# A banded-attention and feed-forward kernel gets a new planner, fixed PSUM pieces, wider loads and a split last tile

## The chip, the cores and the metric

The kernel runs on one core of a Trainium2 chip. The metric is the device time of one execution in microseconds (us). The engines named below are TensorE (PE in the profile, PEld for its weight loads), VectorE (DVE), ScalarE (ACT), GpSimd (POOL) and the sync engine (SP), which only issues transfers. Each engine works through its own instructions in the order in which they were emitted.

## The reference

Attention over 4 sequences of 768 tokens, 8 heads of 64, each query seeing the 96 tokens up to itself and the first 8 tokens of the sequence, with a bias that falls with distance at a slope of its own per head; then a feed-forward layer without skip:

```python
scores = scale * np.matmul(q, k.transpose(0, 1, 3, 2))
keep = is_global | is_local                       # first 8 tokens, or 0 <= rel < 96
dist = np.where(is_global & ~is_local, 96.0, np.abs(rel))
scores = np.where(keep, scores - slopes * dist, -1e9)
a = softmax(scores)
x = (a @ v) as 3072 rows of 512
h = x @ w_in                                      # 512 -> 2048
out = (h - np.tanh(h)) @ w_out                    # 2048 -> 512
```

All inputs and the output are float32; the kernel's matmuls take bfloat16.

## The kernel before, in words

**Tiles.** The 3072 tokens are 24 tiles of 128 tokens, six to a sequence. A tile needs the keys of itself and of the tile before it, so it has two score blocks, `o=0` (diagonal) and `o=1` (off-diagonal); the first tile of a sequence has only the diagonal one, which makes 44 blocks. The 8 global keys and values are copied into the first rows of each later tile (`a_K`, `a_V`), so that the off-diagonal block covers them too.

**One tile's way.** `load` fetches k, q and v (256 KB each, line 143) by SP. `cast` (line 157) turns k and q to bfloat16, on GpSimd except for tile 0. k and q are transposed: for tiles 0 to 7 by TensorE (`a_T`, line 169, eight 128x128 transposes into one PSUM bank) with copies out by ScalarE and VectorE (`a_Te`, 180 and 182), from tile 8 on by a transposing transfer (`a_DT`, line 173). `a_S` (line 190) makes one block of scores: 8 matmuls of 128 columns, one per head, into a two-bank PSUM piece. `a_E` (198, ScalarE) takes the exponential; `a_M` (202, VectorE) multiplies it by `mk`, the exponential of bias and mask. `a_AV` (213 and 217) multiplies by v, with a column of ones for the row sums; `a_R` (225 and 226) divides; `a_X` and `a_Xe` (240, 249), from tile 9 on `a_DX` (252), transpose the result into `xT`. So much is the attention.

**The feed-forward part.** `m1` (line 273) multiplies by `w_in` into one PSUM bank, `m1_th` (284, ScalarE) takes tanh, `m1_g` (290, VectorE) subtracts. The first six tiles go one by one (four blocks of 128 columns fill a bank: 16 matmuls of 128 columns), the rest in threes (one block of 384 columns: 4 matmuls). `m2` (300) multiplies by `w_out`, in four quarters of four matmuls of 512 columns; `m2_e` (307) copies out, `store` (310) writes 256 KB.

**Weights.** `w_in` and `w_out` come in four pieces of 1 MB each (lines 149 and 152, issued by GpSimd and cast on the way). Weights and the early tiles share one list, `before`: tiles 0 to 3, the four pieces of `w_in`, the four of `w_out`, then tiles 4, 5, 6. An entry of that list waits for the landing of the one two places ahead of it (except between neighbouring tiles).

**The order.** Every step is put down by `op` with its engine, an assumed duration, what it follows (`after`) and which buffers it takes and gives. `plan` walks through them: again and again it takes the step that can start first, with a priority for ties, and so fixes the order on each engine before anything runs. m1 and m2 (priority 2) fill up TensorE. `with_warm` then adds matmuls on zeros (`warm`, line 265) wherever TensorE is planned idle up to 19 us. PSUM is two pools: two pieces of two banks, shared by score blocks and AV results, and four single banks for all else; a pool hands out its pieces in turn.

**The start.** Ahead of the planned steps, VectorE builds the distances and masks in `rmat` (lines 92 to 104) from a GpSimd iota and sets the ones of v, and ScalarE makes `mk` of it by 8 exponentials (line 107).

Of the kernel before, what the change touches and what calls it, by code (L numbers as in the profile page):

```python
# [8 lines left out]
FP32 = mybir.dt.float32  # L9
# [7 lines left out]
def kernel(  # L17
# [30 lines left out]
    PE_T, PE_X = 8, 9  # L48
    HT = 3


    EARLY, EARLY2 = 6, 4
# [17 lines left out]
    ident = cpool.tile([P, P], BF16, name="ident")  # L70
    mk = cpool.tile([P, H, 3, P], BF16, name="mk")
    rmat = cpool.tile([P, 3, P], FP32, name="rmat")
    tmp01 = cpool.tile([P, 2, 2, P], FP32, name="tmp01")
# [4 lines left out]


    def slot(h):  # L80
        return (h % 2) * NP + h // 2


    def build_masks():


        r = rmat[:, 1:3, :]
# [5 lines left out]
            out=tmp01[:, 0], in0=r, scalar1=0.0, scalar2=BIG, op0=ALU.is_lt, op1=ALU.mult  # L93
        )
        nc.vector.tensor_scalar(
            out=tmp01[:, 1], in0=r, scalar1=float(L), scalar2=BIG, op0=ALU.is_ge, op1=ALU.mult
        )
        nc.vector.tensor_tensor(out=r, in0=r, in1=tmp01[:, 0], op=ALU.max)
        nc.vector.tensor_tensor(out=r, in0=r, in1=tmp01[:, 1], op=ALU.max)
# [4 lines left out]
        nc.vector.memset(rmat[0:G, 2, :], float(L))  # L104
        for h in range(H):
            slope = 2.0 ** (-8.0 * (h + 1) / H)
            nc.scalar.activation(mk[:, slot(h), :, :], rmat, AF.Exp, bias=0.0, scale=-slope)


    ops = {}  # L110
    w_in_r = moe_w_in.rearrange("(c p) f -> p c f", p=P)
    w_out_r = moe_w_out.rearrange("(c p) d -> p c d", p=P)
    PE, ACT, DVE, POOL, SP = ENG.PE, ENG.Activation, ENG.DVE, ENG.Pool, ENG.SP

    LAT = {PE: 0.17, ACT: 0.1, DVE: 0.1, POOL: 0.12, SP: 0.0}

    def op(key, eng, us, fn, after=(), take=(), give=(), pri=0, dma=0.0):
        ops[key] = dict(
            key=key, eng=eng, us=us, fn=fn, after=[a for a in after if a is not None],
            take=list(take), give=list(give), pri=pri, dma=dma,  # L120
        )

# [12 lines left out]


    kf, qf, vf = {}, {}, {}
    kq = {}

    def load(u, nm, src, dst):  # L140
        b, i = u // NQ, u % NQ
        dst[u] = stpool.tile([P, H, Dh], FP32, name=nm)
        started(("ld", nm, u), nc.sync.dma_start(  # L143
            out=dst[u], in_=src[b, :, i * P : (i + 1) * P, :].rearrange("h p d -> p h d")
        ))
# [410 lines left out]
```

## Time and profile before

| | |
|---|---|
| runs | 225.67 us median of 3 (224.74 to 227.08) |
| profiled execution, first to last instruction | span 224.4 us; its time with what lies around the span is not listed |
| TensorE busy | 211.9 us, 94% of the span; 11.5 us of it on zeros (line 265) |
| VectorE, ScalarE, GpSimd busy | 136.4, 124.2, 53.8 us |
| first feed-forward matmul | 21.44 us |
| last matmul to the end | 220.8 to 224.4 us |

A busy TensorE is the union of its matmuls' spans, so time lost between matmuls that overlap isn't seen in it; the start-to-start time is read from the chain. The profile's waits name what ended an engine's idle time.

### The profile page before, as it was taken

The page shows a single profiled execution, that of the slowest core. Times are in us where ns is not written, and L with a number is a line of the kernel's source. Part 1 is how long each engine was busy: PE and PEld are TensorE (multiplying, and loading weights), DVE is VectorE, ACT ScalarE, POOL GpSimd, SP SyncE. Part 2 cuts the span into 40 slices and gives each one's busy share as a digit, 9 for nine tenths or more (in the row PEclk, how much of TensorE's full clock was granted, in tenths as well). Part 3 has the DMA queues.
Part 4 walks back from the last instruction along what each step waited for, and adds up shares of the span by engine and source line. Part 5 has one row for each costly group of instructions (what it writes and reads, how often), then busy time and mean ns, then how long its engine had stood idle before and what let it go on. Part 6 is the DMA issues. An engine that isn't in the chain of part 4 may idle for free.

```text
span 224.4 us, 5020 instructions
## 1 busy us (share of the span) xinstructions
PE 211.9 (94%) x1975; PEld 126.0 (56%) x1998; DVE 136.4 (61%) x279; ACT 124.2 (55%) x205; POOL 53.8 (24%) x85
## 2 busy tenths in 40 slices
PE   6898899999899999899999999999999999999993
PEld 2455897555785565445555555555555555555541
DVE  5367785215898599743897767677675743444300
ACT  5655654256775487543778384746664644544321
POOL 1473212064463432233233332322000000000000
PEclk9999999999999999999999999999999999999999
DMA  7999999999999999999999999997514121011112
GB/s 151 219 207 152 151 191 164 221 204 290 240 190 201 189 265 194 193 200 196 250 240 198 206 187 234 223 170 150 120 33 107 50 70 47 3 48 47 47 49 95
DMA packets 107640, 35.85 MB, mean 160 GB/s; under 512 B 100448, under 2 KB 104544, under 8 KB 107616
## 3 DMA queue, kind: packets, MB, share of 16 engines
q1 hardware_dynamic: 103392, 31.34, 72.3%
q0 software_dynamic: 4224, 4.19, 12.1%
q8 instruction: 15, 0.25, 0.5%
q14 instruction: 9, 0.07, 0.1%
HBM read 27.26 MB, written 6.29 MB: 150 GB/s over the span
## 4 chain that ended last, share of the span: by engine, by line
PE 78%; DMA 7%; SPq 6%; DVE 3%; ACT 3%; issue 1%
PE one L273 35%; PE one L300 34%; SPq L143 5%; PE big L190 4%; DMA w_in_bf_97<-in_moe_w_in_dram 3%; DMA vf<-in_v_dram 3%; PE big L213 2%; PE big L217 2%; DMA xT<-x 2%; ACT pd L198 2%; DVE po L202 1%; DVE pd L202 1%; PE one L240 1%; PE one L169 1%; DVE xT L249 1%
## 5 line engine op out<-in xcount | busy, mean ns | idle before, releaser
L284 ACT ACTIVATE th<-one 128x384 f32<-128x384 f32 (+1 forms) x120 | 60.7, 516 | 51.7 <-PE one L273 47.7
L290 DVE TENSOR_TENSOR g<-one,th 128x384 bf16<-128x384 f32 (+1 forms) x120 | 67.6, 579 | 32.7 <-ACT th L284 30.7
L300 PEld LDWEIGHTS <-g 128*128 128x128 bf16 x384 | 36.0, 98 | 36.0
L198 ACT ACTIVATE pd<-big 128x1024 bf16<-128x1024 f32 x24 | 24.6, 1024 | 16.6 <-PE big L190 14.9
L157 POOL CAST kq<-kf 128x512 bf16<-128x512 f32 x23 | 14.8, 645 | 56.7 <-DMA kf<-in_k_dram 46.6
L307 ACT COPY ot<-one 128x512 f32<-128x512 f32 x24 | 14.1, 587 | 23.9 <-PE one L300 23.8
L202 DVE TENSOR_TENSOR pd<-pd,mk 128x1024 bf16<-128x1024 bf16 x24 | 18.4, 768 | 11.9 <-ACT pd L198 11.5
L273 PE MATMUL one<-xT,w_in_bf_96 128*128 128x128 bf16 (+1 forms) x192 | 24.6, 273 | 1.1 <-DVE xT L249 0.9
L273 PE MATMUL one<-xT,w_in_bf_97 128*128 128x128 bf16 (+1 forms) x192 | 24.7, 273 | 0.8 <-DMA w_in_bf_97<-in_moe_w_in_dram 0.8
L273 PE MATMUL one<-xT,w_in_bf_99 128*128 128x128 bf16 (+1 forms) x192 | 25.2, 273 | 0.0
L273 PE MATMUL one<-xT,w_in_bf_98 128*128 128x128 bf16 (+1 forms) x192 | 25.1, 273 | 0.0
L300 PE MATMUL one<-w_out_bf_100,g 128*128 128x512 bf16 x88 | 24.1, 379 | 0.5 <-issue 0.2
L300 PE MATMUL one<-w_out_bf_103,g 128*128 128x512 bf16 x94 | 24.1, 379 | 0.2
L300 PE MATMUL one<-w_out_bf_101,g 128*128 128x512 bf16 x92 | 23.8, 379 | 0.2
L300 PE MATMUL one<-w_out_bf_102,g 128*128 128x512 bf16 x89 | 23.1, 379 | 0.4 <-issue 0.2
L198 ACT ACTIVATE po<-big 128x1024 bf16<-128x1024 f32 x20 | 20.5, 1025 | 1.4 <-PE big L190 1.4
L273 PEld LDWEIGHTS <-w_in_bf_96 128*128 128x128 bf16 x192 | 14.6, 98 | 9.1 <-issue 1.3
L273 PEld LDWEIGHTS <-w_in_bf_99 128*128 128x128 bf16 x192 | 14.8, 98 | 7.4
L273 PEld LDWEIGHTS <-w_in_bf_97 128*128 128x128 bf16 x192 | 14.4, 98 | 7.9 <-DMA w_in_bf_97<-in_moe_w_in_dram 1.0
L273 PEld LDWEIGHTS <-w_in_bf_98 128*128 128x128 bf16 x192 | 14.6, 98 | 7.2
L157 POOL CAST kq<-qf 128x512 bf16<-128x512 f32 x23 | 15.6, 678 | 10.0 <-DMA qf<-in_q_dram 9.9
L202 DVE TENSOR_TENSOR po<-po,mk 128x1024 bf16<-128x1024 bf16 x20 | 15.9, 797 | 3.0 <-ACT po L198 3.0
(91 smaller groups left out, 181.2 us busy)
## 6 DMA issues: line engine op xcount, KB each, us to landing
kf<-in_k_dram SPq DMA_DIRECT2D x24, 256.0 KB, 4.0
qf<-in_q_dram SPq DMA_DIRECT2D x24, 256.0 KB, 4.4
vf<-in_v_dram SPq DMA_DIRECT2D x24, 256.0 KB, 4.8
out_dram<-ot SPq DMA_DIRECT2D x24, 256.0 KB, 2.9
w_in_bf_96<-in_moe_w_in_dram POOLq DMA_DIRECT2D x1, 512.0 KB, 6.4
w_in_bf_97<-in_moe_w_in_dram POOLq DMA_DIRECT2D x1, 512.0 KB, 6.5
w_in_bf_98<-in_moe_w_in_dram POOLq DMA_DIRECT2D x1, 512.0 KB, 6.6
w_in_bf_99<-in_moe_w_in_dram POOLq DMA_DIRECT2D x1, 512.0 KB, 5.3
```

What stands on the lines that cost most here:

```text
L143: started(("ld", nm, u), nc.sync.dma_start(out=dst[u], in_=src[b, :, i * P : (i + 1) * P, :].rearrange("h p d -> p h d")))
L157: eng.tensor_copy(out=kq[u][:, j, :], in_=src.pop(u).rearrange("p h d -> p (h d)"))
L190: nc.tensor.matmul(s[:, slot(2 * p + hh), :], qk[u - o][r, 1, p, :], qk[u][r, 0, p, :], start=True, stop=True,)
L198: nc.scalar.activation(pr[u, o], s, AF.Exp, bias=0.0, scale=scale)
L202: nc.vector.tensor_tensor(out=pr[u, o], in0=pr[u, o], in1=mk[:, :, m, :], op=ALU.mult)
L213: nc.tensor.matmul(dst, pr[u, 0][:, slot(h), :], vb[u % NV][:, h, :], start=True, stop=last,)
L217: nc.tensor.matmul(dst, pr[u, 1][:, slot(h), :], vb[(u - 1) % NV][:, h, :], start=False, stop=True,)
L273: nc.tensor.matmul(t[:, (f - f0) * n : (f - f0 + 1) * n], w_in_bf[j][:, c, fo : fo + P], xT[b][:, c, o : o + n], start=(c == 0), stop=(c = ...
L284: nc.scalar.activation(h_view(ths[g, f0], g), h_view(hs[g, f0], g), AF.Tanh, bias=0.0, scale=1.0)
L290: nc.vector.tensor_tensor(out=gs[b][:, f0 : f0 + m, o : o + n], in0=h_view(hs.pop((g, f0)), g), in1=h_view(ths.pop((g, f0)), g), op=ALU.su ...
L300: nc.tensor.matmul(os_[u], gs[u // HT][:, f, t * P : (t + 1) * P], w_out_bf[f // FJ][:, f % FJ, :], start=(f == 0), stop=(f == CF - 1),)
L307: nc.scalar.copy(out=ots[u], in_=os_.pop(u))
```

## The change

- **PSUM pieces.** The two pools go. Two fixed pairs of banks (`pairs`) and four fixed banks (`ones`) are allocated once, and the planner itself assigns which piece each step gets (`got`, `bank`).
- **Planner.** `plan` now follows the two queues of transfers (SP's and GpSimd's) as first-in-first-out lists that share the rate by weights, has other durations and latencies, and for a step of the attention on TensorE compares with 0.3 us added to its readiness once feed-forward work has begun (`MARGIN`).
- **Score blocks.** From tile 5 on the first block takes both pairs, and the second takes none and has priority -9; it is planned after the first one's end.
- **Loads.** k and q of tiles 0 to 8 are loaded with 4 tokens (1 KB) per descriptor in place of one (256 bytes); cast and the copies out of the transposes put the rows in order. Those nine tiles (before: eight) are transposed by TensorE, k and q each in a bank of its own, four transposes each.
- **Order of loads.** Tiles 0 to 4, then `w_in` 0 and 1, `w_out` 0 and 1, `w_in` 2, tile 5, `w_out` 2, `w_in` 3, `w_out` 3, tiles 6 and 7; again each waits for the entry two places ahead.
- **Bias.** In tiles 0 and 1 (three blocks) TensorE adds bias and mask to the scores by 8 matmuls more a block (`a_B`), and `a_M` is left out there. `mk` is made by eight planned steps on ScalarE. The diagonal mask is made on GpSimd (`affine_select`), and the ones of v are set by GpSimd.
- **Last tile.** Its `w_out` product is made in two halves of 256 columns, copied out by ScalarE and VectorE and stored apart.
- **Matmuls on zeros.** The planner's limit goes from 19 to 16 us; 18 are emitted where there were 42.

```diff
-    ps_big = ctx.enter_context(tc.tile_pool(name="ps_big", bufs=2, space=bass.MemoryType.PSUM))
-    ps_one = ctx.enter_context(tc.tile_pool(name="ps_one", bufs=4, space=bass.MemoryType.PSUM))
+    pairs = [psum.tile([P, 2, 512], FP32, name=f"pair{i}") for i in range(2)]
+    ones = [psum.tile([P, 512], FP32, name=f"one{i}") for i in range(4)]
...
+        if nm != "v" and u < PE_T:
+            s = src.rearrange("(a c) (t j) d -> t a c (j d)", c=2, j=J4)
+            i = nc.sync.dma_start(out=t.rearrange("p (c j) d -> p c (j d)", c=2), in_=s)
...
+    def a_Te(u, j, eng):
+        b = half(ones[bank(("T", u, j))])[:, 0 : NP * P]
+        i = b.rearrange("p (j t a) -> p a t j", j=J4, a=NP)
+        o = qk[u][:, j].rearrange("p a (t j) -> p a t j", j=J4)
...
+    def a_B(u, o):
+        s = scores(u, o)
+        for h in range(H):
+            nc.tensor.matmul(
+                s[:, slot(h), :], sid[:, h, :], rbf[:, dist_of(u, o), :],
+                start=(slot(h) % NP == 0), stop=False, skip_group_check=True,
+            )
...
-    AHEAD = 5.0
-    WARM = (1.4, 19.0)
-    before = [("t", 0), ("t", 1), ("t", 2), ("t", 3), ("in", 0), ("in", 1), ("in", 2), ("in", 3),
-              ("out", 0), ("out", 1), ("out", 2), ("out", 3), ("t", 4), ("t", 5), ("t", 6)]
+    AHEAD = 5.5
+    WARM = (1.3, 16.0)
+    MERGE = 5
+    SEQ = ["t0", "t1", "t2", "t3", "t4", "i0", "i1", "o0", "o1", "i2", "t5", "o2", "i3", "o3", "t6", "t7"]
+    LAG = 2
...
+            both = u >= MERGE and i
+            for o in (0, 1) if i else (0,):
+                take = [("pair", ("S", u, 0)), ("pair", ("S", u, 1))] if both else [("pair", ("S", u, o))]
+                take = [] if both and o else take
+                deps = te + [("K", u - 1) if o and i >= 2 else None, ("S", u, 0) if o else None]
...
+                op(("S", u, o), PE, (0.24 if both else 0.4) if o or both else 0.4, lambda u=u, o=o: a_S(u, o),
+                   after=deps, take=take, pri=-9 if both and o else 0)
...
+                late = r
+                if o["eng"] is PE and o["pri"] == 0 and first_m[0] is not None and r > 0:
+                    late = r + MARGIN
+                c = (round(max(f, late), 3), o["pri"], n)
...
+    def l2(qq, c):
+        for f in range(qq * 4, qq * 4 + 4):
+            nc.tensor.matmul(
+                ones[bank(("l2", 0, c))][:, 0:HC], gs[u // HT][:, f, u % HT * P : (u % HT + 1) * P],
+                w_out_bf[f // FJ][:, f % FJ, c * HC : (c + 1) * HC], start=(f == 0), stop=(f == CF - 1),
+            )
```

More of the change, by code (lines that the diff above doesn't have):

```diff
@@ L419, in plan @@
[L419 to L426 removed]
+    make_ops()
+    BUFS = {"pair": 2, "one": 4, "mo": 3, "sk": 4, "sq": 4, "sv": 4, "kq": 3, "p0": 3, "p1": 3,
+            "x": 3, "xT": 4, "g": 3, "th": 3, "ot": 4}
@@ L427, in plan @@
+    START = {PE: WARM[0], ACT: 2.1, DVE: 3.3, POOL: 3.3, SP: 0.75}
+    LAT = {PE: 0.21, ACT: 0.04, DVE: 0.06, POOL: 0.06, SP: 0.0}
+    MARGIN = 0.3
+    RING = 3 * 1024
+    def plan():
+        avail = {n: [(0.0, i) for i in range(c)] for n, c in BUFS.items()}
+        free = dict(START)
+        done = {("dist",): 3.2}
+        start = {}
+        avail["one"][3] = (WARM[1], 3)
+        fifo = {SP: [], POOL: []}
+        clock = [0.0]
         f1 = f2 = 0.0
         queues = {}
-        for u in range(NU):
+        for u in range(NU - 1):
```

515 lines of the change are left out of this document (319 added, 196 removed).

## The prediction

> **What bounds the kernel now.** I read the page's shares first, then busy time by stage, then the waits, the order of time and the chain.
>
> ```profile
> span 224.4 us, 5020 instructions
> PE 211.9 (94%) x1975; PEld 126.0 (56%) x1998; DVE 136.4 (61%) x279; ACT 124.2 (55%) x205; POOL 53.8 (24%) x85
> ...
> L265 PE MATMUL one<-zero 128*128 128x512 bf16 x40 | 11.5, 425 | 1.4 <-DVE zero L514 1.2 <-issue 0.2
> ...
> 15.00:20.00 5.00, 4.27 (x54) 2.46 (x52) 3.66 (x9) 2.62 (x3) 3.30 (x5) 1.00 1.06 163
> 20.00:25.00 5.00, 3.79 (x74) 3.22 (x73) 3.90 (x9) 3.15 (x4) 0.75 (x2) 1.00 1.09 174
> 50.00:60.00 10.00, 8.90 (x134) 6.54 (x132) 6.29 (x13) 7.02 (x10) 5.06 (x7) 1.00 1.16 272
> 60.00:70.00 10.00, 9.64 (x160) 7.84 (x158) 9.72 (x19) 5.78 (x9) 4.17 (x6) 1.00 1.13 190
> 80.00:100.00 20.00, 18.75 (x190) 10.56 (x191) 15.06 (x33) 12.61 (x22) 5.63 (x10) 1.00 1.20 208
> 140.00:160.00 20.00, 19.84 (x171) 11.04 (x173) 13.84 (x28) 13.11 (x22) 5.20 (x7) 1.00 0.93 178
> ...
> 21.44 1.96 PE L273 MATMUL one<-xT,w_in_bf_96 128*128 128x128 bf16 x32
> ...
> PE one L273 <- DMA w_in_bf_97<-in_moe_w_in_dram: 0.8, 1, 0.8
> PE big L217 <- DVE po L202: 1.2, 3, 0.7
> ...
> 220.82 0.59 ACT ot L307
> ```
>
> TensorE bounds it. In a settled stretch (140 to 160 us) it idles 0.16 us in 20, the background that I expect of any plan. So the span splits in four: 21.44 us until the first feed-forward matmul, of which 11.5 us are matmuls on zeros; the work after that; the waits in it; and 3.6 us from the last matmul (220.8) to the end. The waits: 0.8 us for the second piece of w_in, 1.10 + 0.36 us between 50 and 70 us, and 1.25 us between 80 and 100 us, where a value product stands at the head of TensorE until the masked scores (line 202) are ready. The profiled execution's own time isn't listed, so the sum is made on its span; the median of the runs lies 1.27 us above that, and I add the sum to the median.
>
> **The change part by part.**
>
> *First feed-forward matmul.* It waits for the first piece of w_in, which waits for a tile to land.
>
> ```profile
> 6.45 0.61 POOL L160 CAST vb_104<-vf 128x512 bf16<-128x512 f32 x1 [4.83 <-DMA vf<-in_v_dram]
> 10.07 0.73 POOL L160 CAST vb_105<-vf 128x512 bf16<-128x512 f32 x1 [0.60 <-DMA vf<-in_v_dram]
> 13.93 0.88 POOL L149 DMA_DIRECT2D w_in_bf_96<-in_moe_w_in_dram  x1 [0.84 <-DMA vf<-in_v_dram]
> 18.19 0.75 POOL L149 DMA_DIRECT2D w_in_bf_97<-in_moe_w_in_dram  x1 [1.25 <-DMA vf<-in_v_dram]
> 20.59 0.74 POOL L149 DMA_DIRECT2D w_in_bf_98<-in_moe_w_in_dram  x1 [1.04 <-DMA w_in_bf_96<-in_moe_w_in_dram]
> ...
> 27.53 0.74 POOL L152 DMA_DIRECT2D w_out_bf_100<-in_moe_w_out_dram  x1 [1.80 <-DMA w_in_bf_98<-in_moe_w_in_dram]
> 30.55 0.74 POOL L152 DMA_DIRECT2D w_out_bf_101<-in_moe_w_out_dram  x1 [2.29 <-DMA w_in_bf_99<-in_moe_w_in_dram]
> 33.59 0.74 POOL L152 DMA_DIRECT2D w_out_bf_102<-in_moe_w_out_dram  x1 [2.29 <-DMA w_out_bf_100<-in_moe_w_out_dram]
> ```
>
> Tiles land 3.62 us apart (6.45 to 10.07), 1.21 us per 256 KB in pieces of 256 bytes. No row has 1 KB pieces on SP's queue. Upper bound 1.21 us (a larger piece has no reason to cost more); lower bound the weights, whose 1 MB lands every 3.03 us, 0.76 us per 256 KB. I take 0.8, nearest the weights, also long pieces. A tile then takes 0.8 + 0.8 + 1.2 = 2.8 us: the first lands at 5.65, the fourth at 14.05, the fifth at 16.85. The first w_in piece now waits for the fourth tile instead of the third, so it is issued at 14.05 where it was 13.93, and with the same 6.66 us lands near 20.6. The first matmul goes from 21.44 to about 20.6: **-0.8** (from -1.5 to +2.5, the last if the wide loads cost 1.21). The Trainium skill, "DMA: Bandwidth & Descriptors", section Specifications, wants at least 512 bytes per descriptor for full rate; at its 27 GiB/s per engine 256 KB would take an estimated 0.57 us, which would put the fourth tile at about 12.2 us.
>
> What else could be late then is ScalarE.
>
> ```profile
> 0.74 1.28 ACT L107 ACT_TABLE_LOAD   x1 [0.74 <-PEq L537]
> 3.75 3.41 ACT L107 ACTIVATE mk<-rmat 128x384 bf16<-128x384 f32 x8 [1.72 <-DVE rmat L104]
> L198 ACT ACTIVATE pd<-big 128x1024 bf16<-128x1024 f32 x24 | 24.6, 1024 | 16.6 <-PE big L190 14.9 <-DVE vb_106 L232 1.8
> L180 ACT COPY qk<-one 128x512 bf16<-128x512 bf16 x8 | 4.7, 583 | 1.1 <-PE one L169 1.1
> ```
>
> In the changed program the table load waits for VectorE's distances (about 3.1 us), where it ran free at 0.74; behind it queue all ScalarE work. Up to the fifth tile's copy ScalarE has 1.28 + 3.41 + 5 x 0.58 + 7 x 1.02 = 14.7 us, so that copy ends at 17.8 without a gap. The two score blocks of the fifth tile, which stand before the first feed-forward matmul on TensorE, follow it by about 19.5. Weights at 20.6 cover that by 1 us; beyond, each late microsecond is paid. The bias matmuls (three blocks) and the strided copies out fall before 20.6 and replace matmuls on zeros: 0. GpSimd's eight scalings of 128 columns, a quarter each of the 0.61 us that its casts of 512 take (row at 6.45), and eight small memsets are some 2 us ahead of its first cast at 5.65: 0; at the full 0.61 us each they would push that cast by 2 us, into ScalarE's margin.
>
> *TensorE work after that point.* By the emitted orders, before has 38 score blocks left in 26 runs; after has 35 blocks in 35 runs. So "in one run" isn't what comes out: the second block is planned after the end of the first, and feed-forward work that can start sooner slips between each pair. What a run costs:
>
> ```profile
> 36.34 0.86 PE one L300 x4
> 37.20 0.89 PE one L273 x16
> ...
> 48.96 0.55 PE big L190 x16
> 49.52 0.97 PE one L300 x4
> ...
> 57.77 0.33 PE big L190 x8
> 58.10 1.00 PE one L273 x16
> ```
>
> One block takes 0.33 us, two together 0.55, and the group behind any run takes 0.11 more (0.97 for 0.86, 1.00 for 0.89). So a block costs 0.22 and a run 0.22 on top. Nine runs more, +1.98; three blocks fewer, -0.66; one transpose of x fewer (4 x 0.0556), -0.22. Four tiles' q and k transposes remain in both. **+1.1** (0.7 to 1.4).
>
> *The second w_in piece.* Issued when the fifth tile lands (16.85), it is through 3.0 us behind the first, 23.6. TensorE has until then three groups of 16 on piece one (2.7) and two value products: the 0.8 us wait goes, **-0.8**.
>
> *The third w_in piece.* It used to be third, now two w_out pieces are ahead of it. w_out 0 is issued at 20.6 and lands at 26.6 (27.53 to 33.59 was 6.06), the third w_in piece is issued then and lands at 32.7. TensorE until then has ten groups of 16 (8.9), two value products (0.5 each), two transposes of x and one quarter of w_out (0.86), 11.2 us from 20.6, plus some 0.4 us of waits for banks, since VectorE's subtractions stand in a line with divisions there. It arrives at 32.2. Wait 0.5 + 0.4, **+0.9** (0 to +4: tile 5's loads start near 30 and share the rate).
>
> *Starvation at 50 to 70 us.*
>
> ```profile
> 39.24 0.37 SPq L143 DMA_DIRECT2D kf<-in_k_dram  x1
> ```
>
> Tile 4 was first asked for at 39.24. Now tiles 4 and 5 come before that, and tile 6 starts when w_in 3 has landed, near 41. A tile's feed-forward work is 4 x 0.89 + 4 x 0.86 = 7.0 us (rows of the chain above), two tiles 14, less the 1.8 us later start: 12 us more cover. 1.46 - 0.16 of background: **-1.3** (0 to -1.4).
>
> *80 to 100 us.* The waits on line 202 total 1.2 us. The new planner prefers filler where attention would be less than 0.3 us ready, with TensorE's latency set longer; that is about the size of each wait but the longest. But a tile now holds both pairs from its first block. Between nothing and -1.1 I take **-0.6**.
>
> *Tail.*
>
> ```profile
> DMA to landing us min/median/max: 2.0/2.9/4.5
> 1.86 0.29 DVE L95 TENSOR_SCALAR tmp_94<-rmat 128x256 f32<-128x256 f32 x1
> ```
>
> Copy 0.59, then 3.0 us for the last store. Half the columns on VectorE take about 0.3 (256 columns took 0.29), half the bytes between 2.0 and 3.0, say 2.7. **-0.6** (-0.2 to -1.3). The first half hides under the second's matmuls.
>
> Sum: -0.8 + 1.1 - 0.8 + 0.9 - 1.3 - 0.6 - 0.6 = **-2.1**; span 222.3, and 225.67 - 2.1 = **223.6**. The new order from 100 us on I cost at nothing: there TensorE idles so little that it can hardly gain, and other engines have the cover of their shares above (61%, 55%, 24%); should it lose, that is part of the forecast's upper side.
>
> **The rivals.**
>
> 1. *The new order waits nowhere.* The 0.9 doesn't come, the waits at 80 to 100 us go fully (-0.5 more), and the last store is as short as the shortest one (-0.7 more): -4.2, 221.5. For it: 0.16 us per 20 us in settled stretches shows TensorE can be kept so. Against: piece three arrives by my sum later than it is wanted.
> 2. *The wide loads buy nothing* (1.21 us each). Fourth tile at 17.3, first piece at 23.9, first matmul 3.3 us later than forecast: +1.2, 226.9. Against it: the weights' 0.76.
> 3. *TensorE runs dry at piece three, and the clock falls.*
>
> ```profile
> 1.20 3.63 PE L265 MATMUL one<-zero 128*128 128x512 bf16 x9 [1.20 <-DVE zero L514]
> 5.94 1.89 PE L265 MATMUL one<-zero 128*128 128x512 bf16 x8
> ```
>
> The first matmuls of 512 columns come 0.43 us apart, those after 5 us 0.216. If tile 5's loads go ahead of piece three by a whole tile (2.8 us), TensorE stands 3.4 us; the pieces behind are late by as much, about 1.5 us more; and if the clock then falls to the rate of the first row, the next 3.6 us do half work, 1.8 us. -2.1 + 2.8 + 1.5 + 1.8 = +4.0, 229.7. It decides when piece three lands after 35.5 us. For it: 18 matmuls on zeros where there were 42, in-order weights. Against: an even share would cost only a third of it. The Trainium skill, "TensorE: Matmul & The Clock Gate", Part 1, says that an idle window of about 3.4 us halves the clock until about as long a busy one has passed; the two rows agree with the ramp, no row here shows the fall.
>
> **How the numbers follow.** Forecast 0.46 (222.3 to 225.0), rival 1 0.30, rival 2 0.10, rival 3 0.14. Runs differ by 1% among themselves, so 1% (223.4, 227.9) is about what can be told. Faster: all of rival 1 and nearly half of the forecast, 0.51; slower: rival 3 and, with another loss beside it, a little of rival 2, 0.15; same 0.34. Range 220.5 (rival 1 with the first matmul as early as ScalarE lets it, 19.5) to 227.2 (rival 2), which leaves out rival 3 and a little below.
>
> **What would show it.** First line of m1 at 20 to 21.5 us; a wait of TensorE for the third w_in piece near 32, none for the second; score blocks nearly all in runs of 8 with 0.33 us each in the chain; idle under 0.4 us between 50 and 70; last matmul to end about 3.0 us. I am wrong if k and q land 1.2 us apart, if the granted clock dips after 16 us, or if idle of TensorE between 60 and 200 us is more than 2.5 us.

## The result, and the profile after

The changed kernel takes 225.40 us (median of 20 executions), the kernel before, beside it, 226.49 us (20): a ratio of 0.9944, 95% interval 0.9918 to 0.9969, or 1.1 us less. The forecast was 223.6 us, which stands on a median of before of 225.67 from three executions; over twenty that median is 0.8 us higher. So of the 1.8 us by which the forecast misses, 0.8 us is its base, and 1.0 us is the change: -2.1 forecast, -1.1 measured. Executions more than 1.5% above the fastest of their kernel are left out of every median and ratio below.

The profiled execution of the changed kernel took 223.85 us, 1.75 us of it around the span. It is one of the quick ones: in 39 executions of this kernel in four sets the span lay 20 times between 222.0 and 222.9 us and 19 times between 223.3 and 224.7, so that two executions of one program can differ by more than what is to be explained; below, the clock of TensorE is shown to be one reason.

From the page, span and shares:

```profile
span 222.1 us, 5129 instructions
PE 213.5 (96%) x2022; PEld 127.1 (57%) x2022; DVE 135.6 (61%) x269; ACT 124.9 (56%) x206; POOL 56.1 (25%) x102
```

The span is 2.3 us shorter than before's 224.4, close to the -2.1 of the sum. The terms are another matter. Busy time by stage of the changed kernel (stretch, its length, then busy time of PE, PEld, DVE, ACT and POOL, the granted clock, the transfers' share and rate):

```profile
15.00:20.00 5.00, 3.89 (x63) 2.42 (x62) 3.75 (x10) 3.50 (x6) 4.00 (x6) 1.00 0.96 163
20.00:25.00 5.00, 3.62 (x75) 2.90 (x75) 4.56 (x11) 4.31 (x6) 1.48 (x2) 1.00 1.14 183
50.00:60.00 10.00, 10.00 (x144) 7.46 (x142) 6.55 (x13) 7.52 (x12) 3.75 (x7) 1.00 0.86 209
60.00:70.00 10.00, 10.00 (x129) 6.17 (x127) 7.96 (x19) 5.11 (x7) 4.77 (x8) 1.00 1.03 217
80.00:100.00 20.00, 20.00 (x172) 10.11 (x171) 11.50 (x24) 10.73 (x18) 5.53 (x10) 1.00 1.05 211
140.00:160.00 20.00, 20.00 (x173) 10.92 (x172) 13.27 (x29) 10.85 (x20) 3.69 (x6) 1.00 0.70 153
```

The waits of before between 50 and 70 us and between 80 and 100 us are gone altogether; all but 0.2 us of what TensorE still waits for lies ahead of 25 us. Its waits by what ended them (us in total, times, longest):

```profile
PE one L295 <- DVE x L281: 1.2, 2, 0.7
PE pair L232 <- POOL sid L131: 0.8, 3, 0.3
PE pair L242 <- ACT qk L213: 0.8, 1, 0.8
...
PE one L327 <- DVE g L346: 0.2, 1, 0.2
```

No wait for a piece of the weights is among them. In the changed kernel line 242 makes scores, 327 is the first feed-forward product, 354 the second, 203 the transposes of k and q and 295 that of the result x, 232 the bias product, 131 the scaling of the identity for the bias; 213 (ScalarE) and 215 (VectorE) copy k and q out, 281 divides, 346 subtracts tanh; 174 and 176 load `w_in` and `w_out`. GpSimd in order of time (start, duration):

```profile
3.25 4.80 POOL L131 TENSOR_SCALAR sid<-ident 128x128 bf16<-128x128 bf16 x8
8.12 0.61 POOL L191 CAST vb<-sv 128x512 bf16<-128x512 f32 x1
...
14.93 0.95 POOL L174 DMA_DIRECT2D w_in_bf<-in_moe_w_in_dram  x1 [0.76 <-DMA sv<-in_v_dram]
...
20.76 0.74 POOL L176 DMA_DIRECT2D w_out_bf<-in_moe_w_out_dram  x1 [1.76 <-DMA w_in_bf<-in_moe_w_in_dram]
23.61 0.74 POOL L176 DMA_DIRECT2D w_out_bf<-in_moe_w_out_dram  x1 [2.11 <-DMA w_in_bf<-in_moe_w_in_dram]
...
32.37 0.74 POOL L176 DMA_DIRECT2D w_out_bf<-in_moe_w_out_dram  x1 [4.92 <-DMA w_in_bf<-in_moe_w_in_dram]
```

An entry of the list waits for the landing of the one two places ahead, so these rows tell when the pieces of `w_in` land: 20.76, 23.61 and 32.37 us, where 20.6, 23.6 and 32.7 were forecast. But the first feed-forward matmul comes 3 us after its weights. TensorE in order of time:

```profile
22.26 0.40 PE L242 MATMUL pair<-qk 64*128 64x128 bf16 x8 [0.75 <-ACT qk L213]
23.10 0.40 PE L295 MATMUL one<-ident,x 128*128 128x128 bf16 x4 [0.44 <-DVE x L281]
23.43 0.40 PE L242 MATMUL pair<-qk 64*128 64x128 bf16 x8
23.76 1.07 PE L327 MATMUL one<-xT,w_in_bf 128*128 128x128 bf16 x16
```

It stands behind the fifth tile's score blocks, which wait 0.75 us for ScalarE's copy, and behind the transpose of the third tile's x, which waits 0.44 us for VectorE's division. Against the four parts of the span:

| part | before | after | forecast | measured |
|---|---|---|---|---|
| to the first feed-forward matmul | 21.44 | 23.76 | -0.8 | +2.3 |
| from there to the last matmul's end | 199.35 | 195.15 | -0.7 | -4.2 |
| from there to the end | 3.6 | 3.2 | -0.6 | -0.4 |
| span | 224.4 | 222.1 | -2.1 | -2.3 |

The sum came out because two large errors offset each other. The experiments ask whether they belong together, and why many executions are longer than this one.

### The profile page after: what moved, and what is told of

It reads as the page before. It is cut to its first block, busy times and chain, and to the rows that moved or that the text cites. A ratio compares the mean times of both kernels' runs of the same rounds, so it can differ in the third digit from the quotient of the medians.

```text
span 222.1 us, 5129 instructions
## 1 busy us (share of the span) xinstructions
PE 213.5 (96%) x2022; PEld 127.1 (57%) x2022; DVE 135.6 (61%) x269; ACT 124.9 (56%) x206; POOL 56.1 (25%) x102
## 4 chain that ended last, share of the span: by engine, by line
PE 91%; POOL 3%; DVE 2%; issue 1%; ACT 0%; POOLq 0%; DVEq 0%
PE one L327 38%; PE one L354 36%; PE pair L242 6%; PE pair L268 3%; PE pair L272 2%; POOL sid L131 2%; PE one L203 2%; PE one L372 2%; PE one L319 1%; PE one L295 1%; DVE x L281 1%; PE pair L232 1%; ACT po L249 0%; DVE qk L215 0%; DVE vb L287 0%
## 5 line engine op out<-in xcount | busy, mean ns | idle before, releaser
L327 PE MATMUL one<-xT,w_in_bf 128*128 128x128 bf16 (+1 forms) x768 | 97.8, 273 | 0.2 <-DVE g L346 0.2
L354 PE MATMUL one<-w_out_bf,g 128*128 128x512 bf16 x368 | 92.5, 380 | 0.0
L327 PEld LDWEIGHTS <-w_in_bf 128*128 128x128 bf16 x768 | 57.4, 98 | 28.4 <-issue 0.3
L249 ACT ACTIVATE pd<-pair 128x1024 bf16<-128x1024 f32 x24 | 24.6, 1023 | 11.6 <-PE pair L242 11.6
L249 ACT ACTIVATE po<-pair 128x1024 bf16<-128x1024 f32 x20 | 20.5, 1023 | 3.0 <-PE pair L242 2.6
L191 POOL CAST vb<-sv 128x512 bf16<-128x512 f32 x24 | 15.1, 630 | 22.6 <-DMA sv<-in_v_dram 19.2
L242 PE MATMUL pair<-qk 64*128 64x128 bf16 x352 | 17.7, 221 | 1.1 <-ACT qk L213 0.8
L281 DVE TENSOR_TENSOR x<-pair,rden 128x512 bf16<-128x512 f32 x24 | 16.6, 692 | 0.8
L268 PE MATMUL pair<-vb,pd 128*128 128x65 bf16 x192 | 14.4, 196 | 0.2 <-ACT pd L249 0.2
L268 PEld LDWEIGHTS <-pd 128*128 128x128 bf16 x192 | 12.8, 99 | 2.1
```

What stands on the lines that cost most here:

```text
L191: nc.gpsimd.tensor_copy(out=vb[u % NV][:, :, 0:Dh], in_=st.pop(("v", u)))
L242: nc.tensor.matmul(s[:, slot(2 * p + hh), :], qk[u - o][r, 1, p, :], qk[u][r, 0, p, :], start=u >= NB, stop=True, skip_group_check=u < NB,)
L249: nc.scalar.activation(pr[u, o], scores(u, o), AF.Exp, bias=0.0, scale=scale)
L268: nc.tensor.matmul(dst, pr[u, 0][:, slot(h), :], vb[u % NV][:, h, :], start=True, stop=last,)
L281: nc.vector.tensor_tensor(out=xs[u].rearrange("q (a h) d -> q a h d", a=2), in0=t[:, :, :, 0:Dh], in1=rden.to_broadcast([P, 2, H // 2, Dh] ...
L327: nc.tensor.matmul(t[:, (f - f0) * n : (f - f0 + 1) * n], w_in_bf[j][:, c, fo : fo + P], xT[b][:, c, o : o + n], start=(c == 0), stop=(c = ...
```

## Experiments

Ratios are to the kernel before on the same chip. Kernels that stood beside each other are named as such; from set to set the unaltered changed kernel alone moved between 0.987 and 0.994.

**The late start: scalings on VectorE.** (sid_dve)

```diff
-        nc.gpsimd.tensor_scalar(
+        nc.vector.tensor_scalar(
...
-                op(("sid", h), POOL, 0.16, lambda h=h: build_sid(h), after=[("dist",)], pri=-3)
+                op(("sid", h), DVE, 0.1, lambda h=h: build_sid(h), after=[("dist",)], pri=-3)
```

> The changed kernel with one edit: the eight scalings of the identity that feed the bias matmuls are made by VectorE instead of GpSimd. In the changed kernel each took 0.6 us on GpSimd (3.25 to 8.05 us), its first cast came at 8.12 us, and the first feed-forward matmul at 23.76 us although the first w_in piece had landed by 20.76 us. Theory: these scalings alone hold the whole start back; then the first cast comes at about 6 us, the first feed-forward matmul at 20.8 to 21.5 us, and the time falls by 2 to 3 us, to 222.5 to 223.5. Rival: the start is late because TensorE runs at half clock until 11.6 us and ScalarE has its table load behind VectorE; then the first feed-forward matmul moves by less than 0.7 us and the time by less than that.

Measured: ratio 0.9895 (0.983 to 0.996), four spans of 222.4 to 222.7 us. From its order of time:

```profile
3.38 0.89 DVE L131 TENSOR_SCALAR sid<-ident 128x128 bf16<-128x128 bf16 x8
18.04 0.50 PE L203 MATMUL one<-ident,kq 128*128 128x128 bf16 x4 [0.91 <-POOL kq L186]
23.24 1.89 PE L327 MATMUL one<-xT,w_in_bf 128*128 128x128 bf16 x16
```

The eight scalings take VectorE 0.89 us where they took GpSimd 4.80, and the first cast comes at 6.65 instead of 8.12. Yet the first feed-forward matmul comes at 23.24, only 0.5 us earlier, and the span is not shorter than that of the quick executions of the changed kernel. In this profile the clock is at half from 18.2 to 25.0 us, and from the first feed-forward matmul to the last matmul's end it takes 196.0 us, 0.8 more than in the changed kernel's. Ahead of that, GpSimd's two casts for the fifth tile take 1.04 and 1.14 us, where they take 0.63 and 0.69 in the changed kernel, and TensorE waits 0.91 us for the first of them. The other three executions, at a mean clock of 1.000, are no shorter, so the fall of the clock alone doesn't explain the missing gain.

**The matmuls on zeros: more of them.** (warm, with the unaltered kernel beside it as again.) The limit goes to 21 us; 24 are emitted instead of 18. The limit also keeps a bank from the planner longer, but in the two traces the order of the work on TensorE, ScalarE and GpSimd is the same.

```diff
-    WARM = (1.3, 16.0)
+    WARM = (1.3, 21.0)
```

> The changed kernel with matmuls on zeros up to 21 us as the only edit: 24 in place of 18, the rest of TensorE's order the same; the scalings stay on GpSimd. Theory (the clock is half of the loss, GpSimd's scalings the other half): median 0.5 to 1.2 us under the changed kernel's in this set, first feed-forward matmul still at 23 us or later. Rival (the clock alone is the cause): the whole gain of scalings on VectorE with zeros, 2 to 3 us, comes from the zeros.

> The changed kernel once more, as the yardstick of this set on the same chip. Its first profile had the clock full from 11.6 us and a span of 222.1, and its twenty runs fell into spans of 222.0 to 222.6 and 223.5 to 224.6. Theory (the clock falls in some executions): any execution over 223.4 has a mean granted clock under 1, and a profile of such a one shows a half-clock stretch between 15 and 28 us. Rival: the two groups don't go with the clock.

Measured: warm 0.9883 (0.9857 to 0.9909), spans 222.3, 222.3, 222.5 and 223.1; again 0.993 (0.9905 to 0.9954), spans 223.3 to 224.7, none shorter. Warm's first feed-forward matmul comes at 22.92. All 19 executions of the unaltered kernel over 223.2 us have a mean granted clock under 1, as expected, but so have 15 of the 20 shorter ones: the mean doesn't part the two groups. The profile of again is one of a long execution. Two of its stretches, and its first feed-forward group:

```profile
20.00:24.00 4.00, 2.62 (x54) 1.82 (x48) 3.68 (x10) 3.33 (x4) 1.23 (x2) 1.00 1.10 169
24.00:27.50 3.50, 3.11 (x35) 2.72 (x36) 2.73 (x6) 2.15 (x3) 0.63 (x2) 0.51 1.22 194
```

```profile
25.47 1.89 PE L327 MATMUL one<-xT,w_in_bf 128*128 128x128 bf16 x16
```

From 24 to 27.5 us the granted clock is 0.51, and the group of 16 takes 1.89 us instead of 1.07. But it also comes late, at 25.47 instead of 23.76. That begins earlier, with the bias products of the second tile:

```profile
13.14 0.93 PE L232 MATMUL pair<-rbf,sid 128*128 128x128 bf16 x8
14.01 0.40 PE L242 MATMUL pair<-qk 64*128 64x128 bf16 x8
```

The last matmul ends at 221.54, the span is 224.7.

**The same two again, with both causes removed.** (sid_warm, and as sid_warm2 beside the unaltered again2: both edits above together.)

> The changed kernel with the scalings on VectorE and matmuls on zeros up to 21 us (24 in place of 18; the rest of the order is the same). With the scalings on VectorE alone the profiled execution had TensorE's clock at half from 18.2 to 25.0 us and its first feed-forward matmul at 23.24. Theory (thin work lets the clock fall): the six more matmuls on zeros keep the clock full, the first feed-forward matmul comes at 21.3 to 22.3 us, and the time falls by 1 to 1.5 us from the 224.35 of the scalings alone. Rival (the fifth tile's k, cast only at 16.9 us, and the score blocks that stand before the first feed-forward matmul bind it): it stays at 22.5 us or later and the time is within 0.5 us of 224.35.

> The eight scalings on VectorE and zeros planned up to 21 us, now beside the changed kernel itself on one chip. If the late start and the fall of the clock are what the change lost: 2.2 to 3.0 us under the changed kernel's median, spans 221.5 to 222.5, first feed-forward matmul 21.9. Rival, that the earlier ratio of 0.981 owed something to its chip: 1 us under it or less.

> The changed kernel unaltered, for comparison with the three beside it: 225.4 us, ratio 0.993 to 0.996; first feed-forward matmul at 23.8 where the clock stays full, at 25.5 where it falls between 24 and 27 us.

Measured: sid_warm 0.9808 (0.9748 to 0.9868), spans 221.4 to 222.3; sid_warm2 0.9851 (0.9792 to 0.9911), spans 220.8 to 224.3, median 223.77 us; again2 0.9868 (0.9827 to 0.9909), five of six spans 222.0 to 222.5, median 224.12 us. So sid_warm2 and again2, beside each other, differ by 0.35 us, well inside the intervals, against the 2.2 to 3.0 us expected. Again2 is the counterpart of again: the same program with the clock full where it matters. The same stretches, and its first feed-forward group:

```profile
20.00:24.00 4.00, 2.42 (x48) 1.70 (x47) 3.69 (x8) 3.45 (x5) 0.74 (x1) 1.00 1.19 173
24.00:27.50 3.50, 3.50 (x79) 3.50 (x76) 3.15 (x8) 2.29 (x5) 1.45 (x2) 1.00 1.18 167
```

```profile
24.01 1.07 PE L327 MATMUL one<-xT,w_in_bf 128*128 128x128 bf16 x16
```

And the bias products of its second tile:

```profile
12.43 0.61 PE L232 MATMUL pair<-rbf,sid 128*128 128x128 bf16 x8
12.97 0.40 PE L242 MATMUL pair<-qk 64*128 64x128 bf16 x8
```

Same program, 2.4 us between the spans (222.3 and 224.7), and both parts of it lie under a halved clock. In again the clock's record begins with full speed at 13.8 us, in again2 it is back by 11.3; so in again the bias products take 0.93 us instead of 0.61, with others like them, and the scores behind them start at 14.01 instead of 12.97. These 1.04 us go on through ScalarE's queue (its exponential of these scores starts at 14.44 and 13.41) and are still there when the third tile's x is transposed (24.39 and 23.35). The second fall, at 24 us, adds 0.4 us ahead of the first feed-forward group and 0.9 from there on.

As for the start, sid_warm shows why an earlier one in itself gives little. Its first feed-forward matmul comes at 21.92, 1.8 us earlier than the changed kernel's, and its last one ends at 219.15, no earlier than the changed kernel's 218.91. Its first feed-forward group, and its two longest waits from 14 to 100 us:

```profile
21.92 1.07 PE L327 MATMUL one<-xT,w_in_bf 128*128 128x128 bf16 x16
...
PE one L327 <- DMA w_in_bf<-in_moe_w_in_dram: 0.9, 1, 0.9
PE pair L242 <- DMA qk<-kq: 0.7, 1, 0.7
```

The 0.9 us stands between 40 and 50 us (a later piece of `w_in`), the 0.7 us between 70 and 80: the kind of wait that the late start had covered. In sid_warm2, the same program, TensorE waits 1.9 us for GpSimd's casts of k and q between 14 and 100 us, in sid_warm 0.6; its first feed-forward matmul comes at 22.52 and its last one ends at 218.81, 0.1 us before the changed kernel's.

**No bias on TensorE.** (nobias; and nosid_warm, beside warm, which also leaves out the scalings and has zeros to 21 us. In nobias the scalings stayed in, against what the expectation says, though nothing reads them. With the bias products gone the planner puts in more zeros: 24 in nobias, 30 in nosid_warm.)

```diff
-    NB = 2
+    NB = 0
```

> The changed kernel without the bias on TensorE: tiles 0 and 1 are multiplied by the mask as all others are, and there are no scalings. Theory (the scalings on GpSimd hold the start back): first cast near 5.8 us, first feed-forward matmul at 20.8 to 21.8 us, time down by 1.5 to 3 us, though three products with the mask on VectorE come back. Rival (the bias matmuls are worth their cost in the first tiles): first feed-forward matmul not earlier than 23 us, time the same or longer.

> The changed kernel without bias on TensorE and without the scalings (tiles 0 and 1 are multiplied by the mask), zeros up to 21 us. Against the scalings on VectorE with the same zeros (ratio to before 0.981). Theory (the bias matmuls are worth little, since the weights bind the first feed-forward matmul at 21 us): ratio 0.980 to 0.986, first feed-forward matmul at 21 to 22 us. Rival (they take three mask products out of the first tiles' path and so matter): first feed-forward matmul a microsecond later or more, ratio 0.987 or more.

Measured: nobias 0.996 (0.9916 to 1.0003), its first feed-forward matmul at 22.98, so the gain that its theory promised didn't come; nosid_warm 0.9865 (0.9836 to 0.9894), beside warm's 0.9883. The first feed-forward matmul of nosid_warm comes at 21.81, 1.1 us before warm's, its last ends at 219.57, 0.4 us after warm's 219.13; again the earlier start is given back, 1.05 us of it between 40 and 60 us. While the clock holds (full from 6.3 us in warm and 6.7 in nosid_warm) neither the bias products nor GpSimd's scalings cost anything that shows.

**Fewer zeros, nothing else.** (cold, beside the unaltered again3.) The last eight matmuls on zeros are left out at emission; the order on every engine is otherwise the same.

```diff
-            while last + w + 0.1 <= min(t, WARM[1]):
+            while last + w + 0.1 <= min(t, 9.0):
```

> The changed kernel with the same order on every engine, but without its last 8 matmuls on zeros (those planned from 9 us on; 10 are left). If the thin filling before the weights land is what lets the clock fall: the clock falls in every execution and reaches past the first feed-forward matmul more often, spans 223.5 to 226, median 0.5 to 2 us above the changed kernel's beside it. Rival, that the fall comes whatever TensorE is given to do: the same mixture of spans near 222.3 and near 224, median within 0.4 us of the changed kernel's.

> The changed kernel unaltered, on the same chip as the one with fewer zeros: spans in two groups, 222.0 to 222.6 and 223.3 to 224.7, nothing between; median between 224.1 and 225.5.

Measured: cold 225.47 us, 0.9941 (0.9909 to 0.9973), eight of twelve spans over 223.4; again3 224.30 us, 0.9909 (0.9878 to 0.9940), seven of eight spans 222.2 to 222.9, the last 224.0. Beside each other that is 1.2 us for eight matmuls on zeros, which are no work. The medians alone don't prove it: again, the unaltered kernel earlier on the same chip, had 225.44 us. Cold's stretches, in the longest of its twelve executions:

```profile
15.00:20.00 5.00, 3.10 (x53) 2.33 (x54) 3.92 (x8) 2.79 (x5) 4.07 (x6) 0.78 0.93 156
20.00:24.00 4.00, 3.16 (x40) 2.37 (x40) 3.00 (x8) 3.23 (x5) 1.11 (x2) 0.50 1.16 181
24.00:27.50 3.50, 3.26 (x37) 2.87 (x38) 2.58 (x6) 2.00 (x3) 1.01 (x2) 0.50 1.20 188
```

The clock is at half through both last stretches, and the first feed-forward group (at 25.32) takes 1.89 us again. The rival, a fall that comes whatever TensorE is given to do, does not fit the traces: as the last section works out, the clock fell where a stretch of 3.41 us held too little matmul work. Such a stretch finds room between 11.5 and 24 us at a third to a half of its possible places in the three traces of the changed kernel with the clock full there, at 97% in cold's, and at none in warm's or in that of the kernel before. This is a rough estimate from one trace each: sid_dve's gives 87%, while three of its four executions show no fall. The two groups of spans do not part quite as cleanly as expected (222.8 and 222.9 in again3).

**What the wide loads are worth.** (narrow: k and q in pieces of 256 bytes, the planner told so; narrow_plan: the same loads, the planner not told, so that TensorE's order stays the changed kernel's; the latter beside again2.)

```diff
+    U4 = 0
...
-        if nm != "v" and u < PE_T:
+        if nm != "v" and u < U4:
...
-        if u < PE_T:
+        if u < U4:
...
-                four = nm != "v" and u < PE_T
+                four = nm != "v" and u < U4
```

The last pair of lines is in narrow alone; in both, the copies out of the transposes leave out the reordering.

> The changed kernel with k and q of all tiles loaded in pieces of 256 bytes, one token each, as before; all else as in the changed kernel. Theory: five tiles then land 3.6 us apart instead of 2.8, so the fourth lands at about 17.3 instead of 14.9 us, the first w_in piece at about 23.5 instead of 20.8, and the first feed-forward matmul near 24.5 against 23.8, since that was late anyway: time up by 0.5 to 1.5 us. Rival: the wide pieces are worth nothing as long as the start is held back by GpSimd: time the same within 0.4 us.

> k and q of the nine tiles come in 256-byte pieces again, but the planner is told nothing, so the order on TensorE stays that of the changed kernel. If the wide loads are worth what their spacing says (2.9 us a tile against 3.6): the fourth tile lands some 2.7 us later, the first w_in piece is issued at 17.5 instead of 14.9, the first feed-forward matmul comes at 25.5 to 26.5, and the median is 1.5 to 3 us above the changed kernel's (ratio to before 1.001 to 1.008). Rival, that the 3.5% which the narrow loads cost before was wholly the other plan and the start hides the rest: within 0.5 us of the changed kernel.

Measured: narrow 1.0346 (1.0275 to 1.0417); narrow_plan 1.0141 (1.0075 to 1.0207), 230.43 us, 6.3 us above again2, more than twice the highest expectation. Narrow_plan's GpSimd, and TensorE's two longest waits from 14 to 100 us:

```profile
18.58 0.95 POOL L175 DMA_DIRECT2D w_in_bf<-in_moe_w_in_dram  x1 [1.78 <-DMA sv<-in_v_dram]
```

```profile
PE one L204 <- POOL kq L189: 3.7, 3, 2.0
PE one L330 <- DMA w_in_bf<-in_moe_w_in_dram: 2.8, 1, 2.8
```

Lines 189, 204 and 330 there are 186, 203 and 327 of the changed kernel. The first piece is issued 3.4 us later than again2's (15.18), but the first feed-forward matmul comes at 25.40, only 1.4 us after again2's. Most is lost later: TensorE idles 3.7 us between 40 and 60 us, 3.0 us more than the idle that the profile of again2 lists from 24 to 80 us together, and the clock is at half from 22.2 to 29.1 us, which adds to it. Without the wide loads the changed kernel would be slower than the one before.

**The order of loads of before.** (oldseq)

```diff
-    SEQ = ["t0", "t1", "t2", "t3", "t4", "i0", "i1", "o0", "o1", "i2", "t5", "o2", "i3", "o3", "t6", "t7"]
+    SEQ = ["t0", "t1", "t2", "t3", "i0", "i1", "i2", "i3", "o0", "o1", "o2", "o3", "t4", "t5", "t6", "t7"]
```

> The changed kernel with the order of loads of before: tiles 0 to 3, the four w_in pieces, the four w_out pieces, then tiles 4 to 7. Theory (the new order of loads took away the idle of TensorE between 50 and 70 us): TensorE idles 1 to 2 us between 45 and 70 us again, the first w_in piece is asked for about 3 us earlier, the time is 0.5 to 2 us longer than the changed kernel's 225.4. Rival (the earlier tiles in 1 KB pieces suffice): no idle there, and the earlier weights make it faster by 1 us or more.

Measured: 0.9929 (0.9888 to 0.9971). The first feed-forward matmul comes at 19.27, 4.5 us earlier than in the changed kernel; TensorE then idles 0.8, 0.9 and 0.9 us in the stretches 40 to 50, 50 to 60 and 80 to 100, and the last matmul ends at 220.55. By the median the order of loads is worth nothing that can be told.

**Joined score blocks.** (join, and sid_join_warm with the two start edits, the latter beside sid_warm.) The second block is planned after the issue of the first, not its end: 17 runs of 16 matmuls and 10 of 8, in place of 43 runs of which 42 are of 8.

```diff
-                deps = te + [("K", u - 1) if o and i >= 2 else None, ("S", u, 0) if o else None]
+                deps = te + [("K", u - 1) if o and i >= 2 else None, (("issue", ("S", u, 0)) if both else ("S", u, 0)) if o else None]
```

> The changed kernel with one edit: from tile 5 on the second score block may follow as soon as the first is issued, not when it has ended, so the two stand in one run (17 runs of 16 matmuls and 10 of 8, where the changed kernel has 43 of 8). Theory: each run costs 0.22 us beside its blocks, so 16 runs fewer take 3.5 us of TensorE away and the time falls by 2.5 to 3.5 us. Rival: blocks of a tile back to back wait for each other's exponential and hold both pairs of banks, so TensorE gets idle in return; then the time changes by less than 1 us.

> The changed kernel with three edits: scalings on VectorE, joined score blocks, matmuls on zeros up to 21 us. Joining alone gave 223.83 us and a wait for keys at 80 to 100 us of 2.3 us; scalings on VectorE alone gave 224.35. Theory (the gains are in different stages and add): 222 to 223 us. Rival (joined blocks give back on waits what they save): no better than the scalings with zeros.

Measured: join 0.987 (0.9802 to 0.9938), sid_join_warm 0.9843 (0.9789 to 0.9898), sid_warm beside it 0.9808. TensorE's stretch from 80 to 100 us in join, and its waits:

```profile
80.00:100.00 20.00, 17.71 (x172) 10.14 (x167) 15.11 (x32) 12.13 (x22) 5.86 (x9) 1.00 1.13 202
```

```profile
PE one L327 <- DVE g L346: 1.0, 3, 0.6
PE pair L242 <- DMA qk<-kq: 1.0, 1, 1.0
...
PE one L327 <- ACT ot L361: 0.4, 1, 0.4
```

From the first feed-forward matmul to the last one's end join takes 195.17 us, as the changed kernel does, with 2.57 us of idle time where that has 0.17. So 2.4 us of TensorE time are saved and 2.4 us of waits come in their place.

**Margin 0.** (nomargin)

```diff
-    MARGIN = 0.3
+    MARGIN = 0.0
```

> The changed kernel with the planner's 0.3 us of margin set to 0. Theory (the margin took away the idle between 80 and 100 us): waits of TensorE for masks, divisions and tanh come back, 1 to 2 us between 50 and 220 us, and the time is up by 1 to 2 us from 225.4. Rival (the longer latencies and the planned banks did it): idle under 0.5 us there, time the same within 0.5 us.

Measured: 0.9961 (0.9914 to 1.0009). The stretch and the wait that the forecast spoke of:

```profile
80.00:100.00 20.00, 19.19 (x168) 10.52 (x167) 14.81 (x30) 12.11 (x22) 6.07 (x9) 1.00 1.03 204
```

```profile
PE pair L272 <- DVE po L252: 1.2, 2, 0.8
```

Without the margin TensorE idles 0.81 us in that stretch, where before had 1.25 and the changed kernel nothing; it is one wait of 0.8 us on the masked scores (the other 0.4 of the row lies at 20 us). By the median the difference to the changed kernel is inside what its sets differ by; its profile also has the clock at half from 23.4 to 26.8 us.

**The last tile whole.** (whole, and whole2 beside again2. One execution of whole took 751 us, the profiled one, so its profile isn't used.)

```diff
-            lastu = u == NU - 1
+            lastu = False
-        for u in range(NU - 1):
+        for u in range(NU):
```

> The changed kernel with the last tile made, copied out and stored whole, as before. Theory: from the last matmul's end to the end of the span it takes 3.6 us in place of 3.2, and the median is 0.3 to 0.7 us longer than the changed kernel's in this set. Rival: the last store's landing varies by more than that, and nothing is to be seen (within 0.3 us).

> The last tile's w_out product whole again. If the halves are worth what the tail of the changed kernel shows (3.2 us from the last matmul's end to the end, before 3.6): 3.6 to 3.7 us here, and the median 0.3 to 0.6 us above the changed kernel's. Rival, that the second half's store lands as late as a whole one: 3.2 us, no difference.

Measured: whole 0.9945 (0.9902 to 0.9989), whole2 0.9935 (0.9900 to 0.9970), again2 0.9868. The last copies, of whole2 and then of again2:

```profile
219.41 0.59 ACT L361 COPY ot<-one 128x512 f32<-128x512 f32 x1 [2.87 <-PE one L354]
```

```profile
219.19 0.42 DVE L381 COPY ot<-one 128x256 f32<-128x256 f32 x1 [8.46 <-PE one L372]
```

From the last matmul's end to the end it takes 3.9 us whole (219.37 to 223.3) and 3.1 us in halves (219.16 to 222.3): 0.8 us. The medians differ by 1.7 us, which also holds the clock (half of whole2's twelve spans are above 224), so the term is read from the profiles.

## Why the prediction missed

Two steps failed: the price of GpSimd's scalings, which made the start 2.3 us later instead of 0.8 earlier and was made up for behind it, and the zero for what replaces the matmuls on zeros, which is where, as far as the traces show, the 1.0 us missing from the median lies.

**First feed-forward matmul (-0.8): wrong, +2.3.** The loads were right: weights landed at 20.76 (20.6), tiles some 2.9 us apart in sid_dve, where no scaling hides it (2.8). What failed is the cover that the prediction gave to ScalarE: "The two score blocks of the fifth tile ... follow it by about 19.5." They came at 22.26 and 23.43. The step behind that is the one on GpSimd: "GpSimd's eight scalings of 128 columns, a quarter each of the 0.61 us". They take 0.60 us each, as much as a cast of 512 columns, so the first cast starts at 8.12 where 5.65 was forecast. The bound was written down ("at the full 0.61 us each they would push that cast by 2 us") and the wrong end taken. With this cause removed and zeros to 21 us (sid_warm) it starts at 21.92, 0.95 us after its weights (20.97) instead of 3.0; zeros alone (warm) bring it to 22.92, the scalings alone (sid_dve) to 23.24, there with the clock at half from 18.2 us on.

**What followed it (-0.7): wrong, -4.2, and not independent of the first.** The wait for the second piece went, as forecast. The +0.9 for the third piece did not come, because TensorE began 3.2 us later than forecast while the piece landed on time (32.37). The waits of 50 to 70 us went, and those of 80 to 100 us wholly, not by half (-1.25 for -0.6; nomargin puts 0.8 of that down to the margin; of the 1.2 us on line 202 that the prediction counted there, 0.4 lay ahead of 26 us and 0.16 at 116). The sum treated the start and the waits for loads as separate terms. They are one: in sid_warm, nosid_warm and oldseq the first feed-forward matmul is 1.8 to 4.5 us earlier, waits come back between 40 and 100 us, and the last matmul ends at 219.2 to 220.6, not before the changed kernel's 218.9.

**TensorE work (+1.1): sign not settled.** The runs stayed split as forecast, and the chain of the changed kernel shows the price of a split unchanged:

```profile
39.25 0.89 PE one L327 x16
...
42.42 1.00 PE one L327 x16
43.75 0.97 PE one L354 x4
```

Join saves 2.4 us by 16 fewer runs, 0.15 us each, where 0.22 was reckoned. But the whole of it can't be read off: before's 199.35 us hold 5.09 us of listed idle time, which leaves 194.3 of work against 195.0 after (+0.7), while part of that idle time is missing records. So it is in again2, whose 195.15 us are those of the changed kernel to the hundredth, though its trace lists 1.95 us idle. There the second feed-forward product lacks records (342 where the other trace has 368):

```profile
L354 PE MATMUL one<-w_out_bf,g 128*128 128x512 bf16 x342 | 88.4, 379 | 1.6 <-issue 0.5
```

The "background" of 0.16 us in 20 that the prediction subtracted is, at least there, no wait.

**Tail (-0.6): right**, 0.4 us against before, 0.8 us against whole2.

**The clock: costed at nothing, and it is where the gain of many executions goes.** "The bias matmuls (three blocks) and the strided copies out fall before 20.6 and replace matmuls on zeros: 0." The 18 matmuls on zeros in place of 42 appear only as a point for rival 3, whose mechanism, the fall of the clock, did come: not at the third piece of `w_in`, but at several places up to 28 us, and without TensorE running dry. Where the clock is full from some 11.5 us on, as in the profiled execution (11.6) and again2, that costs nothing that shows; where the half clock meets the bias products and later the first feed-forward groups, it costs 2.4 us (again). So "replace matmuls on zeros: 0" holds only at full speed: matmuls on zeros wait for nobody, the bias products stand ahead of scores that ScalarE waits for. The missing 1.0 us has its place in such executions: the first set's median span is 223.65 (225.40 less 1.75), 1.55 us above the profiled 222.1, while before's median (224.74 with the same 1.75 us around the span) lies 0.34 above its profiled 224.4; -2.3 + 1.55 - 0.34 = -1.1. That the fall is one reason is shown within one program, row by row, by again against again2; cold against again3 and warm against again agree with it. That it is the only one is not: sid_warm2 has three spans of 223.2 to 224.3 at a mean clock of 0.992 to 0.999, and these stay open.

**The rivals.** Rival 1's zero waits came true without its time, since they were bought with a late start. Rival 2 was rightly put aside, but its price was too low: narrow loads cost 6.3 us in this order, not 3.3, as the loads of the later tiles starve TensorE too.

**The best version.** sid_warm and sid_warm2 are faster than the kernel before (0.981 and 0.985). That they are faster than the changed kernel is not shown: on the chip where both ran the medians are 223.77 and 224.12.

## What to carry to other kernels

A later start of the bound engine and the waits for loads behind it share one budget: forecast the end from when the last load needed lands, not as a sum of a start and waits. Matmuls on zeros are worth their place right up to the first real stretch of work, since the clock can fall over gaps far shorter than the stretch it then stays down, and what replaces them must not be work that another engine waits for. A small instruction on GpSimd is to be priced at the nearest row of any size, not in proportion to its columns.

## What the hardware showed beyond that

**The clock falls without a long gap.** In again TensorE's longest gap between 18 and 24 us is 1.0 us, and it is busy 2.62 of the 4 us from 20 on, yet the clock is at half for the next 3.4 us; in again2 it is busy 2.42 of the same 4 us and the clock stays full. The Trainium skill, "TensorE: Matmul & The Clock Gate", Part 1, names an idle window of about 3.4 us as the condition, and says that the window runs free of the kernel. The length of the fall and its coming and going between executions agree with that; the condition does not: here a partly filled window was enough.

What parts the two cases is where a grid of 3.41 us lies. Within one trace the clock changes only at whole multiples of 3.41 us from each other (in again at 13.81, 24.05 and 27.46), and the grid lies elsewhere in each execution. I add up the matmuls that start in each stretch of the grid at what they cost at full clock: 0.216 us for 512 columns, in proportion for fewer, and half of that for the 64-row ones of the scores, of which a block of eight costs 0.22 us. Over the 19 traces that record the clock, half clock followed all 29 stretches at full clock with 1.26 us of such work or less, and none of the 1166 with 1.28 or more. In again the stretch from 20.63 us has 1.17, though TensorE shows as busy in 2.02 of it. The bound is read off this kernel's traces alone.

**GpSimd's price for a small operation.** From the groups of the changed kernel (busy time, mean ns of one):

```profile
L131 POOL TENSOR_SCALAR sid<-ident 128x128 bf16<-128x128 bf16 x8 | 4.6, 585 | 0.3
```

A scaling of 128 columns takes 0.585 us, a cast of four times as many 0.61 (the row at 8.12). On VectorE the same scaling takes 0.18 us (sid_dve).
